# Five more idle products in the softmax wait of the first layer's last head group

## The chip, the cores and the metric

The kernel runs on one core of one Trainium2 chip. The metric is device time in microseconds (us): the kernel before has a median of 673.32 us over three runs (673.31 to 673.92). Engines are called PE (TensorE, matmuls; PEld is its weight loading), DVE (VectorE), ACT (ScalarE), POOL (GpSimd) and SP (SyncE, which here issues every transfer). Transfers go from HBM to the on-chip memory (SBUF) over 16 DMA engines. Matmul results land in PSUM.

## The reference

One decoding step through two identical layers. Each layer is attention over a cache of 4096 keys in 32 heads, and then a dense block with a GELU; both add to x.

```python
def _A_ref(x, k_cache, v_cache, wq, wo):        # x [1, 1, 512]; caches [1, 32, 4096, 128]
    q = (x @ wq).reshape(B, Sq, H, Dh).transpose(0, 2, 1, 3)
    scores = einsum("bhqd,bhkd->bhqk", q, k_cache) * (Dh ** -0.5)
    p = softmax(scores, axis=-1)
    o = einsum("bhqk,bhkd->bhqd", p, v_cache)
    return o.transpose(0, 2, 1, 3).reshape(B, Sq, H * Dh) @ wo

def _B_ref(x, w1, b1, w2, b2):                   # F = 1376
    h = gelu(einsum("bsd,df->bsf", x, w1) + b1)
    return einsum("bsf,fd->bsd", h, w2) + b2

for _ in range(2):
    x = x + _A_ref(_layernorm(x), k_cache, v_cache, wq, wo)
    x = x + _B_ref(_layernorm(x), w1, b1, w2, b2)
return x
```

All of it is float32. Both layers use the same caches and weights. The two caches together are 2 x 32 x 4096 x 128 x 4 bytes = 134 MB for one layer.

## The kernel before, in words

The 32 heads are worked on in 8 groups of 4 heads. A group has a block of keys K and a block of values V, each 128 partitions x 16384 numbers (8.4 MB), cut into C = 8 chunks of 128 x 2048 (1.05 MB). The first layer (`layer == 0`) takes the groups 0 to 7, the second takes them 7 to 0, so that what is left in SBUF of group 7 (and a part of group 6) need not be read again. All transfers go through `load` (line 87), which puts them on SP's queue in program order; SP waits there until the place in SBUF is free. Most work on PE and DVE is pinned to program order too.

For one group the order is:

- `scores` (line 232): for each of 8 chunks four matmuls, one per head, each in its own quarter of the PE array's columns, accumulating in the PSUM tile `pS`.
- `softmax`: DVE takes the maximum over `pS` (line 236) and spreads it (lines 240 to 243), ACT computes exp (line 244), PE transposes the probabilities into `pO` (line 246), and DVE copies them into `pt` (line 248).
- Values: in most groups of the first layer ACT and DVE weight the V tiles (lines 269, 274, 279). In the last two groups of that layer, and the first, second and last two of the second, PE multiplies them (`values`, line 262), four matmuls per chunk into `pO`.
- `scaled_out` and the output projection with `wo` (lines 287 to 332), and the query of the next group (`queries`, lines 213 to 223).

In the last group of each layer (`final`) the V block comes in four transfers, chunks 0 to 3, 4 to 5, 6, and 7 (`LAST = ((0, 4), (4, 6), (6, 7))`, and the last chunk by `END_PARTS`). Chunks 0 to 6 go through `values`; chunk 7 goes through `scaled_out_last` (line 299) into `pS`, whose result DVE transposes (line 302). Then `mlp` follows: `hidden` (line 355) multiplies by w1 in three parts as its weights land, ACT applies the GELU (line 382), and PE multiplies by w2 (line 414). In the first layer `mlp` also issues the next transfers (`follow`): after certain w2 chunks the parts of w2 that reuse the place of earlier parts, the next wq, and the first K chunk of the second layer.

`idle` (line 438) is a matmul whose result nobody reads: 8 columns of the identity as weights, and 512 (or 256) columns of a tile that is in SBUF already as the moving operand. It is pinned in program order like the others. With `FILL = 3`, the second layer's last group has three of them into `pO` between `scores` and `softmax`, and two into `pS` between `softmax` and `values`:

```python
    def idle(t, at, n=512):
        pin(nc.tensor.matmul(at[:C, :n], ident[:, :C], t[:, 0, :n], start=True, stop=True))
```

The first layer's last group has them after chunks 3, 5 and 6 of its values (`LAST_IDLE`), and later in `mlp`, but none in the softmax's wait. In the trace a float32 matmul of 512 columns shows as two records, so one `idle` is x2, and the four matmuls of a chunk are x8.

Of the kernel before, what the change touches and what calls it, by code (L numbers as in the profile page):

```python
# [50 lines left out]
FILL = 3  # L51
# [9 lines left out]
def decode_layers(ctx: ExitStack, tc: tile.TileContext, k, v, w, w1, w2, out):  # L61
# [23 lines left out]
    def load(at, src):  # L85
        t = arena[:, at : at + src.shape[-1]]
        tc.keep_in_program_order(nc.sync.dma_start(t, src))  # L87
        return t
# [4 lines left out]
    def chunk(t, i=0):  # L93
        return t[:, NC * i : NC * (i + 1)].rearrange("p (j n) -> p j n", j=4)
# [6 lines left out]
    def wq_at(g):  # L101
        return (g + 1) % 2, g
# [27 lines left out]
    row, _ = wq_at(0)  # L130
# [129 lines left out]
    def values(i, pt, vt, c, of=C):  # L260
        for j in range(J):
            nc.tensor.matmul(pO[32 * j : 32 * j + 4, :], pt[:, j, c, :], by_head(vt)[:, j],  # L262
                             start=(i == 0), stop=(i == of - 1))
# [22 lines left out]
    def scaled_out(rl, ot):  # L286
        nc.vector.transpose(ot[:, :512], pO)  # L287
        diag = ot.rearrange("p (b q) -> p b q", q=129)[:, :, :P]
        diag = diag.rearrange("p b (d q) -> p d b q", q=32)[:, :, :, 0]
        o, on = small("o", 4), small("on", 4)  # L290
        nc.vector.tensor_reduce(o, diag, axis=AX.X, op=ALU.add)
        nc.vector.tensor_scalar(on, o, rl, None, op0=ALU.mult)
        return on
# [132 lines left out]
    def stream(what, g, pieces, base):  # L426

        for a, b in pieces:
            t = load(base + NC * a, part(k if what == "k" else v, g, a, b))
            for c in range(a, b):  # L430
                here[what, g, c] = chunk(t, c - a)
                yield c, here[what, g, c]
# [4 lines left out]
    def idle(t, at, n=512):  # L437
        pin(nc.tensor.matmul(at[:C, :n], ident[:, :C], t[:, 0, :n], start=True, stop=True))  # L438

    for layer in range(2):  # L440
# [23 lines left out]
        for n, g in enumerate(order):  # L464
            first, final = n == 0, n == G - 1
# [32 lines left out]
                late[1]()  # L498
                late = None
            if first or final:  # L500
                for _ in range(FILL if layer == 1 else 0):
                    idle(t, pO)
            p, ot = free_now(layer, n)
            if layer == 1 and first:
# [6 lines left out]
            if layer == 1 and n == 0:  # L511
                for c in range(C):
                    values(c, pt, here["v", g, c], c)
            elif layer == 1 and n == 1:
                for c in range(C):
                    values(c, pt, here["v", g, c], c)

                for pieces, base in ((((0, 4),), K2_HOME), (((4, 6),), SPARE - 4 * NC)):
                    for _ in stream("k", order[2], pieces, base):
                        pass  # L520
            elif final:
                last_v = chunk(arena[:, v_home + BLOCK - NC : v_home + BLOCK])
                for _ in range(FILL - 1 if layer == 1 else 0):
                    idle(t, pS)
                for c, t in stream("v", g, LAST, v_home):
                    values(c, pt, t, c, C - 1)
                    if c == C - 2:
                        others = scaled_out(rl, ot)
                    for _ in range(LAST_IDLE.get(c, 0) * (1 + layer)):
                        idle(t, pS, 512 >> layer)  # L530
                for a, b in END_PARTS[layer]:
                    at = BLOCK - NC + U * a
                    load(v_home + at, v[g][:, at : BLOCK - NC + U * b])
                for c in range(C):
                    here["v", g, c] = chunk(arena[:, v_home + NC * c : v_home + NC * (c + 1)])
            else:
                for c, t in stream("v", g, WHOLE, v_home):
                    for i in range(KEPT - 1):
                        if layer == 0 and n == G - 2 and c == (STAY + U * i) // NC:
                            nc.scalar.copy(pK[i], t[:, STAY // U % J + i - J * (c - STAY // NC), :])  # L540
                    if pairs is None:
                        values(c, pt, t, c)
# [145 lines left out]
```

## Time and profile before

| | |
|---|---|
| median of three runs | 673.32 us (673.31 to 673.92) |
| profiled execution: span from first to last instruction | 671.6 us; no time of its own beside the span is given for this execution, and the median is 1.7 us more than the span |
| bytes read from HBM | 284.92 MB, 424 GB/s over the span |
| share of the 16 DMA engines taken by the transfers' queue | 99.1% |
| busy share of the span: PE, PEld, DVE, ACT, POOL | 45%, 12%, 61%, 32%, 1% |
| mean granted PE clock | 0.713 of full speed (full is 2.4 GHz, half is 1.2 GHz) |

The page cuts the span into 40 slices of 16.8 us and gives in each the busy share of every engine, the granted PE clock, and what the DMA engines did. The chain of waits is followed back from the last instruction to what released it. Where a row says `[0.55 <-DMA arena<-in_v]`, the engine sat idle for 0.55 us before it, and the landing of a transfer from the tensor in_v ended that. `in_k`, `in_v` and `in_w` are the K cache, the V cache and any of the weights; `arena` is the one big SBUF tile that all of them land in.

### The profile page before, as it was taken

The page shows a single profiled execution, that of the slowest core. Times are in us where ns is not written, and L with a number is a line of the kernel's source. Part 1 is how long each engine was busy: PE and PEld are TensorE (multiplying, and loading weights), DVE is VectorE, ACT ScalarE, POOL GpSimd, SP SyncE. Part 2 cuts the span into 40 slices and gives each one's busy share as a digit, 9 for nine tenths or more (in the row PEclk, how much of TensorE's full clock was granted, in tenths as well). Part 3 has the DMA queues.
Part 4 walks back from the last instruction along what each step waited for, and adds up shares of the span by engine and source line. Part 5 has one row for each costly group of instructions (what it writes and reads, how often), then busy time and mean ns, then how long its engine had stood idle before and what let it go on. Part 6 is the DMA issues. An engine that isn't in the chain of part 4 may idle for free.

```text
span 671.6 us, 6013 instructions
## 1 busy us (share of the span) xinstructions
PE 299.7 (45%) x2236; PEld 79.7 (12%) x2236; DVE 407.1 (61%) x510; ACT 215.4 (32%) x697; POOL 5.2 (1%) x26
## 2 busy tenths in 40 slices
PE   1511703415116053165768986704316025065597
PEld 1000100101001010011114311101001001011124
DVE  3059679498696886971322313288597694973513
ACT  0047074190560823802011200083290650910010
POOL 1000000000000000000000000000000000000000
PEclk9965755757558557578689998655757559557799
DMA  9999999999999999999999999999999999999997
GB/s 377 437 437 438 435 437 437 403 461 437 437 437 397 444 426 434 433 429 426 425 415 399 422 422 438 437 433 433 431 433 437 437 430 402 462 426 414 431 414 286
DMA packets 11556, 285.29 MB, mean 425 GB/s; under 512 B 1284, under 2 KB 1288, under 8 KB 3720
## 3 DMA queue, kind: packets, MB, share of 16 engines
q1 hardware_dynamic: 11528, 284.92, 99.1%
q8 instruction: 17, 0.28, 0.2%
q14 instruction: 11, 0.09, 0.0%
HBM read 284.92 MB, written 0.00 MB: 424 GB/s over the span
## 4 chain that ended last, share of the span: by engine, by line
DMA 64%; PE 17%; DVE 15%; issue 1%; another core or an unknown queue 1%; SPq 1%; ACT 0%; DVEq 0%; ACTq 0%
DMA arena<-in_v 37%; DMA arena<-in_k 24%; PE pS L232 8%; DVE arena L274 7%; PE pO L262 5%; DMA arena<-in_w 4%; DVE arena L279 3%; DVE arena L311 2%; PE pO L283 1%; DVE arena L287 1%; DVE arena L215 1%; SPq L87 1%; PE pB L323 1%; DVE arena L309 0%
## 5 line engine op out<-in xcount | busy, mean ns | idle before, releaser
L269 ACT ACTIVATE arena<-arena,pt 128x128 f32<-128x128 f32 x640 | 188.0, 387 | 50.8 <-DMA arena<-in_v 48.1
L232 PE MATMUL pS<-arena,smalls 128*8 128x512 f32 x1024 | 147.0, 727 | 78.4 <-DMA arena<-in_k 74.3
L279 DVE TENSOR_TENSOR arena<-arena 128x4096 f32<-128x4096 f32 x30 | 132.6, 4420 | 0.3
L274 DVE TENSOR_TENSOR arena<-arena,pt 128x2048 f32<-128x2048 f32 x40 | 89.0, 2287 | 36.8 <-DMA arena<-in_v 35.7
L217 PE MATMUL pS<-arena,smalls 128*128 128x512 f32 x20 | 20.7, 1140 | 202.5 <-DVE arena L215 202.5
L244 ACT ACTIVATE arena<-pS,smalls 128x512 f32<-128x512 f32 x16 | 12.4, 777 | 289.4 <-DVE smalls L243 289.4
L287 DVE STREAM_TRANSPOSE arena<-pO 128x512 f32<-128x512 f32 x16 | 11.5, 717 | 97.4 <-PE pO L262 61.9
L262 PE MATMUL pO<-arena,pt 128*4 128x512 f32 x368 | 48.9, 666 | 11.8 <-DMA arena<-in_v 11.0
L232 PEld LDWEIGHTS pS<-arena,smalls 128*8 128x8 f32 x1024 | 29.8, 102 | 198.6 <-issue 177.3
L236 DVE TENSOR_REDUCE smalls<-pS 128x1 f32<-128x512 f32 x16 | 11.0, 687 | 64.1 <-PE pS L232 64.1
L215 DVE SCALAR_TENSOR_TENSOR arena<-arena,smalls 128x512 f32<-128x512 f32 x45 | 33.8, 752 | 1.6
L311 DVE SCALAR_TENSOR_TENSOR arena<-arena,smalls 128x512 f32<-128x512 f32 x39 | 29.3, 752 | 1.4
L217 PEld LDWEIGHTS pS<-arena,smalls 128*128 128x128 f32 x20 | 5.0, 311 | 206.2 <-DVE arena L215 206.2
L315 PE MATMUL pB<-arena,smalls 128*1 128x512 f32 x26 | 14.7, 648 | 29.0 <-DVE arena L311 29.0
L246 PE MATMUL pO<-ident,arena 128*128 128x128 f32 x64 | 13.4, 344 | 28.1 <-ACT arena L244 27.8
L574 DVE TENSOR_TENSOR arena<-arena 128x2048 f32<-128x2048 f32 x10 | 22.9, 2292 | 0.3
L382 ACT ACTIVATE smalls<-smalls 128x4 f32<-128x4 f32 (+1 forms) x6 | 1.2, 205 | 44.0 <-DVE smalls L375 25.6
L262 PEld LDWEIGHTS pO<-arena,pt 128*4 128x4 f32 x368 | 9.8, 93 | 44.8 <-issue 42.4
L250 DVE STREAM_TRANSPOSE smalls<-smalls 128x32 f32<-128x32 f32 x16 | 3.4, 212 | 17.5 <-ACT arena L244 17.5
L246 PEld LDWEIGHTS pO<-ident,arena 128*128 128x128 f32 x64 | 8.4, 167 | 42.1 <-ACT arena L244 36.7
L244 ACT ACT_TABLE_LOAD x1 | 1.3, 1283 | 36.9 <-DVE smalls L243 36.9
L438 PE MATMUL pS<-arena,ident 128*8 128x256 f32 (+1 forms) x34 | 11.9, 454 | 0.5 <-DVE pt L367 0.5
(115 smaller groups left out, 183.6 us busy)
## 6 DMA issues: line engine op xcount, KB each, us to landing
arena<-in_w SPq DMA_DIRECT2D x13, 2048.0 KB, 12.5
arena<-in_k SPq DMA_DIRECT2D x6, 4096.0 KB, 21.3
arena<-in_v SPq DMA_DIRECT2D x2, 4096.0 KB, 25.1
arena<-in_w SPq DMA_DIRECT2D x6, 1024.0 KB, 30.9
arena<-in_v SPq DMA_DIRECT2D x2, 2048.0 KB, 37.0
arena<-in_k SPq DMA_DIRECT2D x2, 2048.0 KB, 13.4
arena<-in_w SPq DMA_DIRECT2D x7, 512.0 KB, 9.3
arena<-in_v SPq DMA_DIRECT2D x3, 1024.0 KB, 46.3
```

What stands on the lines that cost most here:

```text
L215: pin(nc.vector.scalar_tensor_tensor(t, wt[:, c, :], xc[:, c : c + 1], t, op0=ALU.mult, op1=ALU.add))
L217: pin(nc.tensor.matmul(at, one.to_broadcast([P, P]), t, start=True, stop=True))
L232: pin(nc.tensor.matmul(pS[32 * j : 32 * j + C, :], z[:, j, C - 1 - c : 2 * C - 1 - c], kt[:, j, :], start=(c == 0), stop=(c == C - 1)))
L246: nc.tensor.transpose(pT[:, b].rearrange("p j r -> p (j r)"), p[:, P * b : P * (b + 1)], ident)
L262: nc.tensor.matmul(pO[32 * j : 32 * j + 4, :], pt[:, j, c, :], by_head(vt)[:, j], start=(i == 0), stop=(i == of - 1))
L269: nc.scalar.activation(own, own, AF.Copy, scale=pt[:, j, c, b : b + 1])
L274: nc.vector.tensor_tensor(own, own, weight, op=ALU.mult)
L279: pin(nc.vector.tensor_tensor(a, a, b, op=ALU.add))
L287: nc.vector.transpose(ot[:, :512], pO)
L311: pin(nc.vector.scalar_tensor_tensor(t, wt[:, d, :], on[:, d : d + 1], t, op0=ALU.mult, op1=ALU.add))
L315: pin(nc.tensor.matmul(pB[0:1, :], one, t, start=n == 0, stop=n == G - 2))
L574: pin(nc.vector.tensor_tensor(total, total, other, op=ALU.add))
```

## The change

Two conditions. With the change the five idle products are issued in the last group of both layers, where before they were issued in the second layer alone. (The three ahead of the softmax also stand in the second layer's first group, before and now.)

```diff
--- before.py
+++ after.py
@@ -498,7 +498,7 @@
                 late[1]()
                 late = None
             if first or final:
-                for _ in range(FILL if layer == 1 else 0):
+                for _ in range(FILL if layer == 1 or final else 0):
                     idle(t, pO)
             p, ot = free_now(layer, n)
             if layer == 1 and first:
@@ -520,7 +520,7 @@
                         pass
             elif final:
                 last_v = chunk(arena[:, v_home + BLOCK - NC : v_home + BLOCK])
-                for _ in range(FILL - 1 if layer == 1 else 0):
+                for _ in range(FILL - 1):
                     idle(t, pS)
                 for c, t in stream("v", g, LAST, v_home):
                     values(c, pt, t, c, C - 1)
```

PE's instructions at the end of the first layer's last group, before and now (a row is a line of the kernel, the output tile, the operands, the output's shape and how many follow one another; L217 is the group's query, L232 the scores, L246 the transposes of the probabilities, L262 the values):

```order
 L217 MATMUL pO<-arena,smalls 128x512
 L232 MATMUL pS<-arena,smalls 8x512 x32
+L438 MATMUL pO<-arena,ident 8x512 x3
 L246 MATMUL pO<-ident,arena 128x128 x4
+L438 MATMUL pS<-arena,ident 8x512 x2
 L262 MATMUL pO<-arena,pt 4x512 x16
 L438 MATMUL pS<-arena,ident 8x512
```

Three products now stand ahead of the transposes and two ahead of the values; nothing else on PE moved, and on DVE, ACT, POOL and SP the instructions and their order are the same.

The same place in the second layer, on PE, which is alike in both kernels:

```order
L232 MATMUL pS<-arena,smalls 8x512 x32
L438 MATMUL pO<-arena,ident 8x512 x3
L246 MATMUL pO<-ident,arena 128x128 x4
L438 MATMUL pS<-arena,ident 8x512 x2
L262 MATMUL pO<-arena,pt 4x512 x16
```

Here the products stood in the kernel before already, between the same two neighbours.

## Rows read from the trace of the kernel before

**Rows 1.** The page: DMA in 40 slices, and the transfers' queue (packets, MB, share).

```profile
DMA  9999999999999999999999999999999999999997
GB/s 377 437 437 438 435 437 437 403 461 437 437 437 397 444 426 434 433 429 426 425 415 399 422 422 438 437 433 433 431 433 437 437 430 402 462 426 414 431 414 286
...
q1 hardware_dynamic: 11528, 284.92, 99.1%
```

**Rows 2.** The chain of waits, 300 to 372 us: start us, us, what.

```profile
302.12 39.89 DMA arena<-in_v
...
342.14 5.04 PE pO L262 x32
...
351.45 0.75 PE pS L438 x2
```

**Rows 3.** The timeline, first layer's last softmax: start us, us, engine, line [idle before <-releaser].

```profile
333.49 2.75 PE L232 MATMUL pS<-arena,smalls 128*8 128x512 f32 x24
...
339.00 0.66 PE L246 MATMUL pO<-ident,arena 128*128 128x128 f32 x4 [2.76 <-ACT arena L244]
...
342.14 1.89 PE L262 MATMUL pO<-arena,pt 128*4 128x512 f32 x8 [2.48 <-DMA arena<-in_v]
```

**Rows 4.** PE's weight loads, first layer's last values.

```profile
342.95 0.15 PEld L262 LDWEIGHTS pO<-arena,pt 128*4 128x4 f32 x4 [0.70 <-issue]
...
346.57 0.09 PEld L438 LDWEIGHTS pS<-arena,ident 128*8 128x8 f32 x1 [0.33 <-issue]
```

**Rows 5.** PE's weight loads, second layer's last values.

```profile
648.72 0.14 PEld L262 LDWEIGHTS pO<-arena,pt 128*4 128x4 f32 x8 [1.15 <-issue]
649.18 0.11 PEld L262 LDWEIGHTS pO<-arena,pt 128*4 128x4 f32 x4 [0.32 <-issue]
...
651.75 0.09 PEld L438 LDWEIGHTS pS<-arena,ident 128*8 128x8 f32 x1 [0.32 <-issue]
```

**Rows 6.** PE's timeline, second layer's last softmax.

```profile
643.11 2.74 PE L438 MATMUL pO<-arena,ident 128*8 128x512 f32 x6
646.03 0.66 PE L246 MATMUL pO<-ident,arena 128*128 128x128 f32 x4 [0.18 <-ACT arena L244]
646.62 1.88 PE L438 MATMUL pS<-arena,ident 128*8 128x512 f32 x4
```

**Rows 7.** Stretches, first layer: us, each engine's busy (x), PEclk, DMA share, GB/s.

```profile
336.00:338.00 2.00, 0.23 (x4) 0.00 (x0) 1.51 (x5) 0.00 (x0) 0.00 (x0) 1.00 0.91 393
...
340.00:342.00 2.00, 0.00 (x0) 0.00 (x0) 0.09 (x2) 0.45 (x2) 0.00 (x0) 0.91 0.89 377
342.00:344.00 2.00, 1.86 (x12) 0.45 (x16) 0.00 (x0) 0.00 (x0) 0.00 (x0) 0.50 1.04 442
344.00:346.00 2.00, 2.00 (x20) 0.35 (x12) 0.00 (x0) 0.00 (x0) 0.00 (x0) 0.74 0.95 393
...
368.00:370.00 2.00, 1.63 (x50) 0.98 (x46) 0.64 (x3) 0.14 (x1) 0.00 (x0) 1.00 0.95 336
```

**Rows 8.** The same, second layer.

```profile
646.00:648.00 2.00, 1.97 (x8) 0.70 (x8) 1.01 (x6) 1.49 (x2) 0.00 (x0) 1.00 0.94 401
648.00:650.00 2.00, 1.75 (x14) 0.35 (x16) 0.00 (x0) 0.00 (x0) 0.00 (x0) 1.00 1.02 434
```

**Rows 9.** The timeline, where the last V chunk lands.

```profile
351.93 0.96 PEld L299 LDWEIGHTS pS<-arena,pt 128*1 128x1 f32 x32 [0.55 <-DMA arena<-in_v]
351.94 1.25 PE L299 MATMUL pS<-arena,pt 128*1 128x128 f32 x32
...
353.27 0.32 DVE L302 STREAM_TRANSPOSE pt<-pS 128x128 f32<-128x128 f32 x1 [0.54 <-PE pS L299]
```

**Rows 10.** The timeline, where w1's second part lands.

```profile
360.37 1.45 PE L438 MATMUL pS<-arena,ident 128*8 128x512 f32 x4
...
361.90 0.65 PEld L355 LDWEIGHTS pS<-arena,smalls 128*2 128x2 f32 x28 [0.58 <-DMA arena<-in_w]
361.91 0.84 PE L355 MATMUL pS<-arena,smalls 128*2 128x128 f32 x24
```

## The prediction

> **What bounds the kernel now.** I read the page's DMA lines first, because a kernel that decodes one token reads its caches and does little else. The transfers' queue takes 99.1% of the 16 DMA engines, and the 40 slices show no pause [rows 1]. Only the rate moves: most slices have 422 to 438 GB/s, and 399 stands in the slice that holds the end of the first layer (slice 22, 352.6 to 369.4 us). So PE's time counts only where it makes the queue run dry or slow; elsewhere a faster PE waits longer for data.
>
> Next the chain of waits around the change. It waits for in_v until 342.01, goes through PE's values (L262) from 342.14 to the last idle product at 351.45 without a break, and so into the V remainder [rows 2]. Read alone, that says PE is the late one for some 10 us. The granted clock says why it might be slow there: 1.00 at 336, 0.91 in 340 to 342, 0.50 in 342 to 344, 0.74 in 344 to 346 [rows 7]. PE had stood idle for 2.76 us ahead of the transposes and for 2.48 us ahead of the values [rows 3]. That is the stretch the five products fill.
>
> **Part one: three products into pO ahead of the transposes.** The scores' last 24 records start at 333.49 and stand in six groups of four, 0.43 us apart, so PE is free at 333.49 + 6 x 0.43 = 336.07. The transposes start at 339.00, released by ACT's exp [rows 3]: 2.93 us. Three products are six records; in the second layer six take 2.74 us to the end of the last, and the transposes there still wait 0.18 us for ACT [rows 6]. Put at 336.07 they end at 338.81, 0.19 us ahead of exp. Cost on the path: 0. The cover is that 0.19 us, and it holds only at full clock, which the row at 336 shows (1.00).
>
> **Part two: two products into pS ahead of the values.** They start behind the transposes, at 339.66, and take 1.88 us in the second layer [rows 6]: end at 341.54. V lands at 342.01 [rows 2]. Cost: 0, with 0.47 us to spare. What they read (the K tile, the identity) is in SBUF, so they wait for no transfer; pS has been read by exp before the transposes ahead of them could start.
>
> **Part three: the clock.** In the second layer, with the same five products, the granted clock is 1.00 in 646 to 650 [rows 8], and the seven weight-load steps from 648.72 to 651.75 are 0.43 us each [rows 5], (0.11 of load and 0.32 of waiting for the array), as against 0.85 us at half clock in the first (0.15 and 0.70, at 342.95) [rows 4]. I take it that the first layer does the same. Chunks 0 to 3 are eight groups of four records. Before, they start at 342.14 and the loads of the product behind them stand at 346.57, one group ahead, so they end at 347.00: 4.86 us. After: 8 x 0.43 = 3.44 us, ending at 345.58. PE gains 1.42 us here.
>
> **What is late next.** The four V transfers were put on the queue one behind the other, and chunk 7 landed just ahead of L299's weight load at 351.93, which waited 0.55 us for it [rows 9]. From 342.01 to about 351.9 four chunks landed (4 to 7), 2.47 us each. So chunks 4 and 5, one transfer, land at 342.01 + 2 x 2.47 = 346.95, and chunk 6 at 349.4. These are estimates from the two ends. The faster PE comes to chunk 4 at 346.4 (behind its idle product of two records, 0.86 us), and waits to about 347.05. Chunks 4 and 5 are 1.72 us: 348.8; the idle product 0.86: 349.6, chunk 6 is in; 0.86 and one more idle product of 0.86: 351.35. Then L299 waits for chunk 7 as before, to 351.94.
>
> So of 1.42 us the next wait for V takes most, and what remains at L299 is the end of the queue before it. The chain has the last idle product at 351.45 for 0.75 us, so to 352.20 [rows 2], while L299 starts at 351.94 in the parts of the array that the product leaves free [rows 9]. L299's share in the part that is taken comes some 0.2 us late for it. After the change L299 is done about 0.2 us sooner, and with it L302 (353.07 in place of 353.27) and the dense block behind it.
>
> That 0.2 us goes no further than 361.9. There PE waits for w1's second part: the weight load stood idle 0.58 us and a DMA ended it, and the idle products ahead of it (from 360.37, two records of 512 columns at 0.43 us and two of 256 at half that) leave the array free 1.29 us later, at 361.66: 0.25 us of slack [rows 10]. The landing of w1 is set by bytes queued long before, not by PE. From there PE's chain is as before, and so are the transfers that it releases. The sum: 0 on the time, from the span of 671.6 us, which is 1.7 us under the median; I move the median by nothing: **673.3 us**.
>
> **Bounds.** A gain could come only where the queue is not full. One place near is: 368 to 370 us moves 336 GB/s at a DMA share of 0.95 [rows 7]. Against the 399 of its slice [rows 1] the two us lose 0.3 us of transfers, of which the missing share is 0.1 us. If the 0.2 us did reach the transfers released there, it would be a gain of 0.2 at most. Against: products add reading of SBUF beside the transfers. In the second layer 646 to 648, full of idle products, has 401 GB/s and 340 to 342 in the first, with PE empty, 377 [rows 7, 8]; no loss shows. End for end: -0.2 to +0.1 us for the forecast.
>
> **A rule that says otherwise.** The Trainium skill, TensorE: Matmul & The Clock Gate, section Terms, prices time at low clock as that time times what the clock lacks. By it, the stretch at half clock here (0.36 + 2.00 + 1.04 us out of the three rows from 340 to 346) costs 3.4 x 0.5 = 1.7 us, and 671.6 us would be the median after. The trace bears out the size on PE, about 1.4 us; that it is paid on the clock on the wall is what the wait at L299 speaks against. The Trainium skill says in the same page's Part 1 that the number of slow products differs from run to run; one profile cannot show that.
>
> **The rivals.**
> 1. *PE was the bound and the 1.42 us arrive in full.* For: the chain runs on PE from 342.14 to 351.45 without naming a transfer. Against: the 0.55 us that L299's load waited for in_v, and the steady DMA rate. Time 673.3 - 1.4 = 671.9, a gain of 0.21%.
> 2. *The clock falls elsewhere in other executions.* The stretch at half clock begins at 341.6 in the profile and would begin or end elsewhere in another execution. The longest such start in this kernel is not in these rows; if all eight groups were at half clock, chunks 0 to 3 would take 8 x 0.85 = 6.8 us, 1.94 more than the 4.86 here, less the 0.25 of slack at 361.9: up to 1.7 us in one execution, of which the products would save all. Half of that, halfway between none and all, is 0.9: 672.4. It is still inside 0.2%. The three runs, 0.61 us apart, speak against much of it.
> 3. *The products delay the softmax: slower.* If PE's clock is low when the scores end, three products are 6 x 0.85 = 5.1 us, to 341.2 where exp is ready at 339.00: 2.2 us late. The two into pS then need 3.4 us, from 341.9 to 345.3, and the values start 3.2 us late; at full clock they make up 1.42. Some 1.7 to 1.8 us remain at L299, 1.5 behind the slack at 361.9, where the queue is soon shallow: 674.8, or 0.22% slower. It decides as soon as the products end after 339.00, that is from 0.19 us on. Against: 1.00 in 336 to 338 after a run of scores, and the second layer's transposes, which still wait for ACT.
> 4. *The products do not hold the clock.* They are eight columns wide. Then nothing changes: 673.3. Against: rows 8.
>
> **How the numbers follow.** Forecast 0.77, rival 2 with gains under 0.2% 0.10, rival 4 0.04, rival 1 0.04, rival 3 0.05. What a measurement of this kernel can tell from no change is about 0.2%, 1.35 us. So faster 0.04, same 0.91, slower 0.05. The range reaches down to rival 2's 672.4, and up to the forecast's 673.3 + 0.1 and the highest run before it with a margin of its own size, 674.0. Rivals 1 and 3 lie outside.
>
> **What would show it.** In the profile after: the granted clock at 1.00 throughout 336 to 352; three products (six records) between scores and transposes, with the transposes waiting some 0.2 us for ACT; the values' steps at 0.43 us from the first; a new wait of about 0.6 us for in_v ahead of chunk 4; L299 starting at the same 351.9 behind a wait for in_v that is longer than 0.55; L302 some 0.2 us sooner; L355 at 361.9 unmoved, with the wait for in_w longer. The prediction is wrong if L299 starts a microsecond sooner, if the transposes start after 339.0, or if the queue's rate in 366 to 372 rises.

## The result, and the profile after

| | before | after |
|---|---|---|
| median of 22 runs each | 673.87 us (673.18 to 676.17) | 675.25 us (674.53 to 676.00) |
| ratio to before | | 1.0015, 95% interval 1.0010 to 1.0021 |
| profiled execution: span | 671.6 us | 673.0 us |

The kernel became slower by 1.0 us (0.15%) by the ratio, by 1.4 us between the medians: less than the 0.2% that the prediction set as its bound, but clear of noise and above its range (674.0). The lowest run after (674.53) is 1.35 us over the lowest before.

In the stretch that was changed, the profile after looks as predicted. PE's timeline there (start us, us, line, [idle before <-releaser]), which answers to [rows 3, 4, 9]:

```profile
337.14 2.74 PE L438 MATMUL pO<-arena,ident 128*8 128x512 f32 x6
340.08 0.66 PE L246 MATMUL pO<-ident,arena 128*128 128x128 f32 x4 [0.20 <-ACT arena L244]
340.67 1.45 PE L438 MATMUL pS<-arena,ident 128*8 128x512 f32 x3
341.90 0.61 PE L262 MATMUL pO<-arena,pt 128*4 128x512 f32 x3
341.96 0.59 PE L438 MATMUL pS<-arena,ident 128*8 128x512 f32 x1
342.33 3.65 PE L262 MATMUL pO<-arena,pt 128*4 128x512 f32 x29
345.82 1.02 PE L438 MATMUL pS<-arena,ident 128*8 128x512 f32 x2
346.74 1.90 PE L262 MATMUL pO<-arena,pt 128*4 128x512 f32 x16
...
351.69 1.05 PE L299 MATMUL pS<-arena,pt 128*1 128x128 f32 x32 [0.49 <-DMA arena<-in_v]
```

The six records, the 0.20 us that is left for exp, then values without slow steps, and a gap between 345.82 + 0.86 = 346.68 and chunk 4. Two of the stretches, which answer to [rows 7]:

```profile
342.00:344.00 2.00, 2.00 (x21) 0.53 (x18) 0.00 (x0) 0.00 (x0) 0.00 (x0) 1.00 0.98 418
344.00:346.00 2.00, 2.00 (x18) 0.51 (x11) 0.00 (x0) 0.00 (x0) 0.00 (x0) 1.00 0.97 401
```

The granted clock is 1.00 in place of 0.50 and 0.74. And two waits for weights behind it, for wo and for w1, the second of which answers to [rows 10]:

```profile
354.28 1.05 PE L327 MATMUL pS<-arena,smalls 128*1 128x128 f32 x32 [0.29 <-DMA arena<-in_w]
...
361.66 0.76 PEld L355 LDWEIGHTS pS<-arena,smalls 128*2 128x2 f32 x32 [0.58 <-DMA arena<-in_w]
```

Before, L327 started at 354.51 and did not wait for weights. Now both start 0.23 to 0.24 us sooner than before, by as much as the first V transfer of the group landed sooner. So the gain is gone at L327 already, and nothing is lost yet.

The loss is at the very end. The chain's last pieces before (start us, us, what), and after:

```profile
656.04 11.41 DMA arena<-in_w
667.46 0.14 issue
667.59 1.00 PE pO L414 x24
```

```profile
657.11 12.22 DMA arena<-in_w
669.33 0.04 issue
669.37 0.63 PE pO L414 x8
```

PE's last block is the product with w2, 24 records behind the second last w2 transfer, of which the last eight need the last one. Before, they run through, and the weight load of the last eight waits 0.23 us:

```profile
668.15 0.11 PEld L414 LDWEIGHTS pO<-arena,smalls 128*1 128x1 f32 x8 [0.23 <-DMA arena<-in_w]
```

After, 16 run, and eight stand 1.37 us behind:

```profile
667.38 0.62 PE L414 MATMUL pO<-arena,smalls 128*1 128x128 f32 x16 [0.22 <-DMA arena<-in_w]
669.37 0.61 PE L414 MATMUL pO<-arena,smalls 128*1 128x128 f32 x8 [1.37 <-DMA arena<-in_w]
```

667.38 is 0.21 us sooner than the 667.59 of before; then 1.4 us are lost in one wait. The kernel itself asked for nothing else there. But the DMA queues list a second queue, in the profile page of before too: `q8 instruction`, 17 packets of 0.28 MB, 16 KB each. I take them to bring PE's instructions (e2 below, with 256 more, has 18 packets); from here on "a page" is one such packet of instructions. The queue rows of 667.2 to 667.3 us before (packets that start there, MB, share of 16 engines), of 667.1 to 667.2 after, and of 668.2 to 668.3 after:

```profile
q8 instruction: 1, 0.02, 69.3%
q1 hardware_dynamic: 5, 0.01, 22.2%
```

```profile
q8 instruction: 1, 0.02, 67.9%
q1 hardware_dynamic: 6, 0.01, 32.9%
```

```profile
q1 hardware_dynamic: 1, 0.00, 1.5%
```

After, the packet starts at 667.15 and takes 67.9% of 16 x 0.1 us = 1.09 us on one engine, to 668.24. No packet of the kernel's own queue starts between 667.45 and 668.2. At 668.23 the last one does, a few bytes long: the end of the last w2 transfer, which reports it landed. The trace does not name the engine of a packet; that these two share one is read from the two times. Before, the same packet starts at 667.26, only 0.11 us later, but nothing of the last weights waits for it: the kernel's own queue starts its last packet by 667.66. Theory from here on: five products are 20 PE instructions (the trace has 20 records more), and so PE's pages end at another place of the program's end.

### The profile page after: what moved, and what is told of

It reads as the page before. It is cut to its first block, busy times and chain, and to the rows that moved or that the text cites. A ratio compares the mean times of both kernels' runs of the same rounds, so it can differ in the third digit from the quotient of the medians.

```text
span 673.0 us, 6033 instructions
## 1 busy us (share of the span) xinstructions
PE 303.3 (45%) x2246; PEld 80.5 (12%) x2246; DVE 407.0 (60%) x510; ACT 215.3 (32%) x697; POOL 5.2 (1%) x26
## 4 chain that ended last, share of the span: by engine, by line
DMA 63%; PE 17%; DVE 16%; another core or an unknown queue 2%; issue 1%; SPq 0%; ACT 0%; DVEq 0%; ACTq 0%
DMA arena<-in_v 31%; DMA arena<-in_k 23%; DMA arena<-in_w 8%; PE pS L232 8%; DVE arena L274 7%; PE pO L262 5%; DVE arena L279 3%; DVE arena L311 2%; DVE arena L287 1%; PE pO L283 1%; DVE arena L215 1%; PE pB L323 1%; DVE arena L309 1%; SPq L87 0%
## 5 line engine op out<-in xcount | busy, mean ns | idle before, releaser
L232 PE MATMUL pS<-arena,smalls 128*8 128x512 f32 x1024 | 146.0, 723 | 78.1 <-DMA arena<-in_k 73.9
L217 PE MATMUL pS<-arena,smalls 128*128 128x512 f32 x20 | 20.8, 1141 | 204.4 <-DVE arena L215 204.4
L262 PE MATMUL pO<-arena,pt 128*4 128x512 f32 x368 | 49.3, 662 | 9.6 <-DMA arena<-in_v 8.8
L232 PEld LDWEIGHTS pS<-arena,smalls 128*8 128x8 f32 x1024 | 29.6, 102 | 197.4 <-issue 176.9
L217 PEld LDWEIGHTS pS<-arena,smalls 128*128 128x128 f32 x20 | 5.0, 311 | 207.4 <-DVE arena L215 207.4
L246 PE MATMUL pO<-ident,arena 128*128 128x128 f32 x64 | 13.0, 338 | 25.6 <-ACT arena L244 25.2
L262 PEld LDWEIGHTS pO<-arena,pt 128*4 128x4 f32 x368 | 10.0, 92 | 42.7 <-issue 39.4
L438 PE MATMUL pS<-arena,ident 128*8 128x256 f32 (+1 forms) x38 | 13.7, 469 | 0.5 <-DVE pt L367 0.5
L246 PEld LDWEIGHTS pO<-ident,arena 128*128 128x128 f32 x64 | 8.1, 162 | 39.6 <-ACT arena L244 34.1
```

The costliest lines, as they stand in the source:

```text
L217: pin(nc.tensor.matmul(at, one.to_broadcast([P, P]), t, start=True, stop=True))
L232: pin(nc.tensor.matmul(pS[32 * j : 32 * j + C, :], z[:, j, C - 1 - c : 2 * C - 1 - c], kt[:, j, :], start=(c == 0), stop=(c == C - 1)))
L246: nc.tensor.transpose(pT[:, b].rearrange("p j r -> p (j r)"), p[:, P * b : P * (b + 1)], ident)
```

## The experiments

Two theories. **Place**: the products in the last wait, or the clock behind them, cost the time. **Page**: only PE's instruction count matters, since it says where PE's pages end and when the next is fetched. A small product (64 columns of the identity) in the first layer's first group, where PE idles for over 15 us, adds four instructions and nothing else (N stands for how many products):

```diff
-            pt, rl = softmax(sc, nsc, p, held)
+            pt, rl = softmax(sc, nsc, p, held); [pin(nc.tensor.matmul(pS[:C, :64], ident[:, :C], ident[:, :64], start=True, stop=True)) for _ in range(N if layer == 0 and first else 0)]
```

| run | edit | PE instructions against before | median, lowest to highest (runs) | ratio to before (95%) |
|---|---|---|---|---|
| e6 | before, five products fewer | -20 | 673.81, 673.11 to 674.38 (11) | 0.9993 (0.9984 to 1.0003) |
| e4 | the change, five others fewer | 0 | 674.20, 673.30 to 675.91 (10) | 1.0006 (0.9993 to 1.0018) |
| e5, e10 | the change with four | +16 | 674.63, 673.46 to 675.60 (9, the tenth is told below); 674.92, 673.48 to 680.98 (10) | 1.0003 (0.9992 to 1.0015); 1.0020 (0.9998 to 1.0042) |
| e9 | before, N = 4 | +16 | 674.43, 673.31 to 675.99 (10) | 1.0003 (0.9991 to 1.0015) |
| after | the change | +20 | 675.25, 674.53 to 676.00 (22) | 1.0015 (1.0010 to 1.0021) |
| e1 | before, N = 5 | +20 | 674.97, 674.51 to 676.06 (10) | 1.0019 (1.0008 to 1.0029) |
| e11 | before, N = 12 | +48 | 674.67, 674.50 to 674.93 (10) | 1.0005 (0.9995 to 1.0015) |
| e12 | before, N = 40 | +160 | 674.12, 673.91 to 674.84 (10) | 1.0002 (0.9993 to 1.0012) |
| e3 | the change, N = 45 | +200 | 673.99, 673.72 to 674.70 (10) | 1.0000 (0.9990 to 1.0009) |
| e7 | before, N = 59 | +236 | 674.10, 673.73 to 674.69 (11) | 1.0004 (0.9995 to 1.0013) |
| e8 | the change, N = 54 | +236 | 673.97, 673.71 to 675.24 (11) | 1.0001 (0.9992 to 1.0010) |
| e2 | the change, N = 59 | +256 | 674.06, 673.82 to 675.76 (10) | 1.0009 (0.9996 to 1.0021) |

Before had medians of 673.75 to 674.00 beside them (31 to 33 runs, from 673.12). The ratios set ten or so runs against the scatter of before, and only those of the change and e1 are clear of 1; the argument rests on the lowest runs and on the profiles. One of the ten executions of e5, its profiled one, took 1646.82 us, with L232's matmuls at 2954 ns in place of 727; nothing is read from it. The 680.98 of e10 stands alone, its trace is of another run, and its cause is open.

**e1, the count without the place** (N = 5).

> The kernel before, with five small idle products (64 columns of the identity) added in the first layer's first group, behind the softmax, where PE has nothing to do for over 15 us; the last softmax's wait is as before. Theory of the instruction fetch: a 16 KB packet of PE's instructions, which comes at a fixed count of PE instructions, is moved 20 instructions earlier and gets ahead of the last w2 transfer's final 4-byte packet on one DMA engine; so the time is that of the changed kernel, 674.9 to 675.6, 1.0 to 1.5 us over before, and the last w2 wait on PE is about 1.4 us as in the changed kernel. Rival, the place matters (the products in the last wait, or the full clock behind them): the time is that of before, within 0.4 us.

Page holds, place falls: 674.97, and no run under 674.51. But the wait of 1.4 us for the last w2 that I expected is not there: its profile shows another cost in its place. PE, from 668 us:

```profile
668.21 0.95 PE L414 MATMUL pO<-arena,smalls 128*1 128x128 f32 x22 [0.22 <-DMA arena<-in_w]
670.26 0.38 PE L414 MATMUL pO<-arena,smalls 128*1 128x128 f32 x2 [1.10 <-issue]
```

Here all weights had landed, since the last eight records' first six ran. The last two wait for nothing that the profile names. The queue row of 667.7 to 667.8:

```profile
q8 instruction: 1, 0.02, 67.4%
```

The packet ends some 1.08 us later, by 668.9 at the latest, and PE goes on about 1.4 us behind that: the last two matmuls stand in the page that it brings. After the change, too, the load for the last two records begins 1.4 us behind the packet's end (668.24):

```profile
669.61 0.08 PEld L414 LDWEIGHTS pO<-arena,smalls 128*1 128x1 f32 x1
```

So there both costs met, and the page by itself would have brought the same end: without the wait for w2, six of the eight records would have run sooner, but not the last two.

**e2 and e3, the page's length** (N = 59 and 45).

> The changed kernel, with 59 small idle products added in the first layer's first group, so that with the five there are 64 more products than before: 256 PE instructions, which is one 16 KB packet of 64-byte instructions. Theory of the instruction fetch: the last packet comes where it came before, with one packet more in all, so the time is that of before, within 0.5 us. Rival, the place matters: as the changed kernel, 674.9 to 675.6. Rival, any PE instruction more costs time: over 675.6.

> The changed kernel, with 45 small idle products added in the first layer's first group: 200 PE instructions more than before, which is 56 short of a packet. Theory of the instruction fetch: the last packet comes 56 instructions later than before, behind all of the weights, so the time is that of the lower runs of before, 673.0 to 673.9. Rivals as for the 59 products: 674.9 or more.

e2 is as expected (though four of its ten runs are over 675.0) and e3 0.1 us over its range: with 256 instructions more the time is back, and with 200 more as well. A time that falls when 180 or 236 instructions are added to the changed kernel is none that instructions cost by being executed.

**e4, the place without the count.** The same five in the last wait, and five later ones left out:

```diff
         else:
-            idle(fill, pO, 2 * P)
-            idle(fill, pO, 2 * P)
+            pass
+
...
-                    for _ in range(LAST_IDLE.get(c, 0) * (1 + layer)):
+                    for _ in range(LAST_IDLE.get(c, 0) * 2 * layer):
```

> The changed kernel, without five other idle products of the first layer (the three behind chunks 3, 5 and 6 of the last values, and two of 256 columns behind the first part of the dense block): PE's count is that of before. Theory of the instruction fetch: time of before, within 0.5 us. Rival, the place matters: as the changed kernel, 674.9 to 675.6.

Runs from 673.30, as before; the median is 0.45 us over, inside the interval. Its profiled execution (675.91) shows the first cost by itself. PE at the end, and the queue rows of 668.5 to 668.6 and of 669.6 to 670.0:

```profile
668.61 0.62 PE L414 MATMUL pO<-arena,smalls 128*1 128x128 f32 x16 [0.21 <-DMA arena<-in_w]
670.72 0.40 PE L414 MATMUL pO<-arena,smalls 128*1 128x128 f32 x8 [1.50 <-DMA arena<-in_w]
```

```profile
q8 instruction: 1, 0.02, 70.1%
q1 hardware_dynamic: 1, 0.00, 0.6%
```

```profile
q1 hardware_dynamic: 2, 0.00, 7.2%
```

The page's packet takes 1.12 us of one engine from 668.53, and two packets of the last weights start behind it. No record waits for the page; the weights do. So there are two costs: (a) the packet gets ahead of the last weights on their engine, in some runs; (b) the last matmuls stand behind the page's end, in all runs with 20 instructions more.

**e5, e9 and e10, four products.** Four instructions fewer should take (b) away and leave (a). e5 and e10 are the same kernel; e9 has N = 4.

```diff
-                for _ in range(FILL - 1):
+                for _ in range(FILL - 1 if layer == 1 else 1):
```

> The change with one product less: three ahead of the transposes, one ahead of the values (16 PE instructions more than before, 4548 records in place of 4552). Theory, page end: in the runs with five, the last two matmul records of the w2 block stand behind the end of a page of instructions and start 1.4 us after the packet with the next page has ended; four instructions fewer bring them ahead of that end, and the pause among the last eight matmuls goes: about before's time, 673.4 to 674.4. Rival, order on the DMA engine: the packet merely comes too early, and 16 instructions are four fifths of the way: 674.4 to 675.2.

> The kernel before, with four small idle products in the first layer's first group: 16 PE instructions more, as with four in the last wait. Theory, two costs at the end of the program: (a) the packet with PE's last page may land on a DMA engine that still carries the last weights, which happens in some runs and costs 1 to 2.5 us in these; (b) with 20 instructions more the last matmuls themselves stand in that page and PE waits for it in every run. With 16 there is (a) alone, a little more often than before: lowest runs 673.2 to 673.6 as before, a third to a half of the runs over 674.5, median 673.6 to 674.7. If (b) began at 16 already, no run would be under 674.3.

> The change with four products once more, for its profile. Theory: as the four products elsewhere; in the profile the last eight w2 records run without a pause among them, whenever their weights landed. If (b) is there, the last one or two records start over 1 us behind the others.

The lowest runs are 673.46, 673.31 and 673.48, as before, and 1.0 us under the lowest with five; the profile of e10 has all 24 records in one row:

```profile
668.28 0.96 PE L414 MATMUL pO<-arena,smalls 128*1 128x128 f32 x24 [0.22 <-DMA arena<-in_w]
```

So (b) starts between 16 and 20 instructions. The medians of e5 and e10 (674.63 and 674.92) are higher than I expected, and e5's lies in the range of its rival (674.4 to 675.2), since half of the runs or more lie over 674.6, where of before about one in five does. I take these to be runs with (a), more frequent at +16 than at 0; no profile at +16 shows one, and the row of e10 was of a run without it. Why 16 instructions, some 0.2 us, should make so much of it I can't show from these profiles.

**e11 and e12, further into the page** (N = 12 and 40).

> The kernel before, with 12 small idle products in the first layer's first group: 48 PE instructions more, so the page ends some 31 instructions ahead of the last matmul. Theory: PE waits in every run for the page, inside the last 24 records of the w2 block, but the packet is asked for about 0.5 us sooner than with five: lowest run 673.8 to 674.6, median 674.2 to 675.2. Rival, more instructions simply cost time: more than with five, 675.3 or over.

> The kernel before, with 40 small idle products in the first layer's first group: 160 PE instructions more. Theory: the page ends ahead of the place where PE waits for the second last w2 transfer, so the wait for the page lies beside that wait, and the packet comes 2 us sooner, on an engine with much left to carry: lowest run 673.3 to 673.9, median 673.7 to 674.5. Rival, more instructions simply cost time: over 675.5.

As expected, with e12's lowest run (673.91) 0.01 us over its range. PE in e11 from 668 us, and in e12 from 665 us:

```profile
668.22 0.40 PE L414 MATMUL pO<-arena,smalls 128*1 128x128 f32 x8 [0.21 <-DMA arena<-in_w]
669.30 0.62 PE L414 MATMUL pO<-arena,smalls 128*1 128x128 f32 x16 [0.68 <-issue]
```

```profile
665.41 0.71 PE L414 MATMUL pO<-arena,smalls 128*1 128x128 f32 x17
666.65 2.44 PE L414 MATMUL pO<-arena,smalls 128*1 128x128 f32 x71 [0.53 <-issue]
```

The pause moves forward with the count: 2 records ahead of the end with 20 instructions, 16 with 48, 71 with 160, by about half the instructions that were added, since every second one is a matmul record. Counted in the traces from the program's start, the PE record that comes late is the 4546th in e1, e11 and e12 alike, and in e3 too (0.42 us, at 666.41): the page ends at a fixed count, whatever stands there. In the kernel before, the last matmul is the 4529th, so 16 more just fit ahead of that end, and 20 do not. In e12 the pause lies where PE would have waited for weights, and costs little. In e11 the ten runs lie within 0.43 us, none under 674.50, which I take as (b) in every run and (a) in none.

**e6, e7 and e8, what the products are worth.** e6 leaves out of the kernel before what e4 leaves out.

> The kernel before, without five idle products (the three behind chunks 3, 5 and 6 of the first layer's last values, and two of 256 columns behind the first part of its dense block): 20 PE instructions fewer. Theory: the packet with the last page is asked for later still, gets ahead of the last weights less often, and the upper runs of before (674.6 and more) go: median 673.2 to 673.7, 0 to 0.5 us under before. Rival, the idle products hold the clock that the chain needs: 0.5 us or more over before.

> The kernel before, with 59 small idle products in the first layer's first group: 236 PE instructions more, 20 short of a page. Theory: as the 45 products with the change (200 more): 673.6 to 674.1, with no run over 675.

> The changed kernel, with 54 small idle products in the first layer's first group: the same count of PE instructions as the kernel before with 59, so the pages end at the same place at the end of the program, and the two differ in the change alone. Theory: the five products by themselves are worth nothing: the same as the kernel with 59 within 0.3 us. Rival, PE was the bound in the last softmax: 1.0 us or more under it. Rival, the products delay something: 1.0 us or more over it.

e7 and e8 have the same count and differ in the change alone: 674.10 and 673.97. In e7's profile the clock is 0.50 in 342 to 346, and its L302 starts 1.03 us behind that of e8:

```profile
354.16 0.32 DVE L302 STREAM_TRANSPOSE pt<-pS 128x128 f32<-128x128 f32 x1 [0.54 <-PE pS L299]
```

```profile
353.13 0.32 DVE L302 STREAM_TRANSPOSE pt<-pS 128x128 f32<-128x128 f32 x1 [1.00 <-PE pS L299]
```

All of that microsecond is gone at the end: e7's profiled execution took 674.00 us and e8's 674.21. So the five products by themselves are worth 0.1 us between the two medians, which these runs can't tell from 0. e6 has no run over 674.38, as expected, but with one in five in before, eleven such runs come by chance in about one case of twelve; its median is 0.1 us over its range and can't be told from before's: no version is shown to beat the kernel before.

## Why the prediction was wrong

- *Part one*, 0.19 us to spare ahead of exp: 0.20 [rows 3].
- *Part two*, 0.47 us to spare ahead of the values: wrong in place, right in cost. The scores ended 1.07 us later in this execution, so the last pS record started at 341.96 with the values already running. The wait ahead of chunk 4 took that up: put at 0.6 us, it was 0.06.
- *Part three*, the clock: 1.00 throughout, and the values' steps 0.43 us.
- *What is late next*: chunk 4 at 346.74 where 347.05 less this execution's lead of 0.24 makes 346.81; L299 at 351.69, its load's wait for in_v grown from 0.55 to 1.42 us; L302 0.46 us sooner, of which 0.24 is that lead and 0.2 the end of the queue, as said. That 0.2 went in L327's new wait for in_w, 7 us sooner than said, so L355's wait stayed 0.58 where it was to grow.
- *The sum*: "From there PE's chain is as before, and so are the transfers that it releases. The sum: 0 on the time". This step failed. From 362 us up to the landing of the second last w2 transfer the transfers land within 0.35 us of before, but for three at 373 to 375 us that came 0.6 us late and were made up; but PE's instructions are themselves transferred, on the same 16 engines, at places that the count sets. Five products cost nothing by their duration that these runs can tell (e7 and e8) and about 1.3 us by their count (e1). The second queue, 0.2% of the engines, was in the profile page of before and was passed over as small. The sum's start was off as well: 673.32 was the median of three runs, and 22 have 673.87, so 0.55 of the 1.93 us between forecast and result are not the change's. That the loss stayed under 0.2% is luck, since what caused it stands in no term of the sum.
- *The rivals*: 1 and 3 fall with e1, which has the lost time without the change, and with e2 and e8, which have the change without the lost time; against 3 stand the transposes too, which still waited 0.20 us for ACT. 2 is real on PE (e7's 0.50 through 346) and worth nothing that e7's time shows. 4 falls with the granted 1.00.

The Trainium skill, Runtime: NRT & Kernel Launch, section Instruction fetch mechanics, says that instructions are refilled in blocks of 16 KiB, 256 instructions, by DMA, and that crossing into the next block is mostly hidden. The traces agree on the block (17 packets for 0.28 MB; 18 in e2, whose time is that of before with 256 more). They don't agree on hidden for the program's end: PE stood 0.68 us in e11 and 1.10 us in e1.

## What to carry to other kernels

An instruction that is hidden in a wait still moves the page ends in all that follows on its engine: where a kernel ends in a fast burst behind its last transfer, look for the instruction packets in the DMA rows near the end, and test a small slowdown by adding the same number of instructions at a harmless place. Compare versions at equal counts (e7 and e8), or the page's place is measured with the edit. And a faster engine between two waits for the same saturated queue gained nothing here that could be told from 0 (e7 and e8), however clear its slow clock was.

## What the runs showed of the hardware that was not expected

- In e1, e3, e11, e12 and after the change, PE went on 1.3 to 1.5 us behind the end of the packet that brought its page (e11: packet of 69.3% x 1.6 = 1.11 us from 666.88, PE at 669.30).
- A 16 KB packet took 1.1 us of one DMA engine (67.4 to 70.1% of 16 x 0.1 us in the rows above). Where it met the last bytes of a transfer over 16 engines, the wait for that transfer was longer still, 1.37 us after the change and 1.50 us in e4. Part of it is open: after the change PE went on 1.14 us behind the start of the last packet (669.37 against 668.23), before about 0.5 us (668.15 against 667.66 at the latest).
- The kernels with a whole page more or nearly so (e2, e3, e7, e8) have lowest runs of 673.71 to 673.82, 0.6 to 0.7 us over those of before: one packet more may cost that, but it wasn't tried apart.
